# Stacking the high and low halves of a folded 33-token chunk over partitions: one or two matmuls in place of three in a Fourier transform

## The chip, the cores and the metric

The kernel runs on one NeuronCore of a Trainium2 chip. The metric is the device time of one execution in microseconds (us). Five engines work side by side, each through its own instructions in order: TensorE (PE; its weight loads are listed as PEld), VectorE (DVE), ScalarE (ACT), GpSimd (POOL) and SyncE (SP), which issues most of the DMAs.

## The reference

Attention with a causal window of 128 keys, then a mixing layer made of a two-dimensional Fourier transform (its real part is added to the input), a layer norm and a feed-forward net. There are 8 batches of 576 tokens, 8 heads of 64, model width 512, hidden width 2048.

```
scores = scale * np.matmul(q, k.transpose(0, 1, 3, 2))
bias = slopes[:, None, None] * (-np.abs(rel).astype(np.float32))[None, :, :]
mask = (rel >= 0) & (rel < window)
scores = np.where(mask, scores + bias[None], -1000000000.0)
...
attn = attn / (np.sum(attn, axis=-1, keepdims=True) + 1e-09)
return np.matmul(attn, v).astype(np.float32)
...
X = np.fft.fft(x, axis=1)
X = np.fft.fft(X, axis=2)
mixed = np.real(X).astype(np.float32)
u = x + mixed
...
un = (u - mu) / np.sqrt(var + 1e-06)
ch = np.maximum(un @ w_ch1, 0.0) @ w_ch2
return (u + ch).astype(np.float32)
```

## The kernel before

Each batch goes through three stages. **Attention** (`scores`, `halves`, `flip`, `values`) leaves an activation tile `X` of 576 tokens x 512 columns on 128 partitions. **The transform** (`fourier`) folds it by the symmetries of sine and cosine, multiplies along the tokens (`rows`, one column in `middle`) and along the columns (`cols`), and adds the result to `X`; `norm` then normalises. **The feed-forward net** (`ffn`) multiplies by two weight matrices (lines 698 and 712). The net of one batch runs beside attention and transform of the next.

Most matmuls need more precision than fp16 gives. A factor is therefore split into two fp16 numbers, a high half and a low half (what the high half misses), and a product is three matmuls: high x high, low x high, high x low.

In the transform the tokens are folded into three chunks, `KCH = (128, 128, 96)` partitions. For each chunk `fold_b` builds the sums and differences `ab`, `fold_c` writes the high halves `fh` (ACT), `fold_d` the low halves `fl` (DVE) and one column's two halves `a128`. `rows(g)` runs for four groups g of 128 columns, two with cosine and two with sine tables, and takes 3 chunks x 3 matmuls of 289 columns; `middle` takes 3 chunks x 3 matmuls of one column for each of three pieces of its output. The third chunk holds 33 tokens on partitions 0 to 32 and their 32 mirror tokens on 64 to 95; between them lies nothing of use, and the tables repeat the cosine rows and the negated sine rows for the mirror tokens.

For each of the batches 2 to 7 `batch_scales` (line 242) reads q, k and v once more ahead of attention, to find the scale of each. It takes 15 pieces of up to 512 columns through two slots: a DMA by `fetch` (line 253), a square and sum on ACT by `part` (line 257). The two slots mean that the third piece's DMA waits until the first is summed.

The work of all stages is put into a queue with due times (`put`, `after`), and the steps are called in the order of these times. The program is then built with a scheduler that orders the instructions of each engine by a timeline of its own; so a changed instruction can move others on every engine. `ffn` evicts each bank of its first product with a Relu on ACT (line 703) and a second half on DVE (line 704; shown as L158, the helper's line).

Of the kernel before, what the change touches and what calls it, by code (L numbers as in the profile page):

```python
# [11 lines left out]
F16 = mybir.dt.float16  # L12
BF16 = mybir.dt.bfloat16
I32 = mybir.dt.int32
AF = mybir.ActivationFunctionType
ALU = mybir.AluOpType
# [7 lines left out]
NS = 289  # L24
# [14 lines left out]
KCH = (128, 128, 96)  # L39
# [37 lines left out]
def attn_fft_ffn_kernel(  # L77
# [39 lines left out]
    A.dma_start(out=tab1_sb, in_=tab1)  # L117
    A.dma_start(out=tab2_sb, in_=tab2)
    A.activation(misc[:, 12:13], half[:, 0:1], AF.Exp)
    vhs = const.tile([128, 2, 2, 5, 65], F16, name="vhs")  # L120
    G.memset(vhs[:, :, :, :, 64:65].rearrange("p a b c d -> p (a b c) d"), 1.0)
    hbuf = const.tile([128, 4096], F32, name="hbuf")
# [15 lines left out]
    def view(t, off, *dims):  # L138
        return bass.AP(tensor=t.tensor, offset=t.offset + off, ap=[t.ap[0]] + [list(d) for d in dims])
# [353 lines left out]
    def fourier(b, t0):  # L493
        st = {}
# [16 lines left out]
        def fold_b(c):  # L511
            m = KCH[c]
            pm = t2k.tile([128, 1032], F32, name="pm", tag="a4", bufs=3).rearrange("p (a b) -> p a b", a=4)
            V.memset(pm[:m, :, 256:257], 0.0)
            ab = t2k.tile([128, 516], F32, name="abcd", tag="b2")[:, 0:512]
            if c < 2:
                fg = st["fg", c]
                V.tensor_tensor(pm[:, 0:2, 0:256], fg[:, :, 0:256], fg[:, :, 256:512], ALU.add)
                V.tensor_tensor(pm[:, 2:4, 0:256], fg[:, :, 0:256], fg[:, :, 256:512], ALU.subtract)
                ia, ib, ic, id_ = 0, 2, 3, 1  # L520
            else:
                X2 = st["X2"]
                V.tensor_tensor(pm[:m, 0, 0:256], X2[:m, 0:256], X2[:m, 256:512], ALU.add)
                V.tensor_tensor(pm[:m, 1, 0:256], X2[:m, 0:256], X2[:m, 256:512], ALU.subtract)
                ia, ib, ic, id_ = 0, 1, 1, 0
            pmm, abm = pm[:m], ab[:m]
            for (i, j, op, o) in ((ia, ic, ALU.add, 0), (ib, id_, ALU.subtract, 128)):
                s_ = 258 * (j - i)
                V.tensor_tensor(view(abm, o, (256, 2), (1, 128)),
                                view(pmm, 258 * i, (s_ + 1, 2), (1, 128)),  # L530
                                view(pmm, 258 * i + 256, (s_ - 1, 2), (-1, 128)), op)
            st["pm", c], st["ab", c] = pm, ab

        def fold_c(c):
            m, sc = KCH[c], st["sc"]
            fh = st["fh", c] = dft.tile([128, 512], F16, name=f"fh{c}")
            A.activation(fh[:m], st["ab", c][:m], AF.Copy, scale=sc[:m, 5:6])

        def fold_d(c):
            m, sc = KCH[c], st["sc"]  # L540
            fh, ab, pm = st["fh", c], st["ab", c], st["pm", c]
            fl = dft.tile([128, 512], F16, name=f"fl{c}")
            V.scalar_tensor_tensor(fl[:m], ab[:m], sc[:m, 5:6], fh[:m], ALU.mult, ALU.subtract)
            a128 = dft.tile([128, 2], F16, name=f"a128{c}")
            V.tensor_scalar(a128[:m, 0:1], pm[:m, 0, 128:129], sc[:m, 5:6], None, ALU.mult)
            V.scalar_tensor_tensor(a128[:m, 1:2], pm[:m, 0, 128:129], sc[:m, 5:6], a128[:m, 0:1],
                                   ALU.mult, ALU.subtract)
            st["in", c] = fh.rearrange("p (g j) -> p g j", g=4), fl.rearrange("p (g j) -> p g j", g=4), a128

        def rows(g):  # L550
            zp = st["zp", g] = bank(b)
            for c, m in enumerate(KCH):
                for p, (l, t) in enumerate(((0, 0), (1, 0), (0, 1))):
                    T.matmul(zp[:, :NS], st["in", c][l][:m, g], tab1_sb[:m, (0 if g < 2 else 2) + t, c],  # L554
                             start=(c == 0 and p == 0), stop=(c == 2 and p == 2))

        def rows_hi(g):
            zh = st["zh", g] = dft.tile([128, NS], F16, name=f"zh{g}")
# [6 lines left out]
        def middle():  # L565
            gps = st["gps"] = bank(b)
            for j, (j0, mj) in enumerate(SCH):
                for c, m in enumerate(KCH):
                    for p, (t, col) in enumerate(((0, 0), (0, 1), (1, 0))):
                        T.matmul(gps[:mj, j:j + 1], tab1_sb[:m, t, c, j0:j0 + mj], st["in", c][2][:m, col:col + 1],  # L570
                                 start=(c == 0 and p == 0), stop=(c == 2 and p == 2))

        def middle_out():
            gt = st["gt"] = small.tile([128, 2, 3], F32, name="gt")
# [52 lines left out]
        t = t0 + f * 2.6  # L627
# [135 lines left out]
def tables():  # L763
# [20 lines left out]
    def split(t):  # L784
        hi = t.astype(np.float16)
        return hi, (t - hi.astype(np.float64)).astype(np.float16)
# [10 lines left out]
    s = np.arange(NS)[None, :]  # L797
    c1, s1 = trig(t * s, 576)
    c1[289:], s1[289:] = 0.0, 0.0
    c1[320:352], s1[320:352] = c1[256:288], -s1[256:288]  # L800
    tab1 = np.empty((128, 4, 3, NS), np.float16)
    for i, x in enumerate(split(c1 * 2048) + split(s1 * 2048)):
        tab1[:, i] = x.reshape(3, 128, NS).transpose(1, 0, 2)
    j0 = np.arange(128)[:, None]
    ke, ko = np.arange(0, 257, 2)[None, :], np.arange(1, 256, 2)[None, :]
    w = np.ones((128, 1))
# [64 lines left out]
```

## Time and profile before

| | |
|---|---|
| Time, three runs | 1102.3 us median (1100.52 to 1106.19) |
| The profiled execution | 1104.11 us, of which the trace spans 1102.3 us |
| PE busy | 1056.0 us (96% of the span), 9260 matmuls |
| DVE busy | 711.4 us (65%) |
| ACT busy | 581.7 us (53%) |
| POOL busy | 19.8 us (2%) |

The share of busy time is an average over stages that have different limits. Up to some 365 us the engines wait for each other and for DMAs; after that PE is busy without a gap until shortly before the end. Matmuls are pipelined, so the duration of one overlaps the next; the chain that ended last shows what each adds.

### The profile page before, as it was taken

What the parts mean: (1) busy time and instruction counts of PE and PEld (TensorE: products, weight loads), DVE (VectorE), ACT (ScalarE), POOL (GpSimd) and SP (SyncE); (2) the same over time, 40 slices, a digit from 0 to 9 for tenths busy, and PEclk for the clock granted to TensorE, in tenths of its full rate; (3) what the DMA queues carried; (4) which work ended last, traced back from release to release, by engine and by line L of the source; (5) the groups of instructions that cost most, each with busy time, mean ns of one, the idle gap of its engine ahead of it and who ended that gap; (6) DMA issues with size and microseconds to landing.
All of it is one profiled execution on the core that took longest, in us unless ns stands there. A gap on an engine that the chain in (4) does not pass through costs nothing.

```text
span 1102.3 us, 23881 instructions
## 1 busy us (share of the span) xinstructions
PE 1056.0 (96%) x9260; PEld 738.6 (67%) x9260; DVE 711.4 (65%) x2081; ACT 581.7 (53%) x1380; POOL 19.8 (2%) x59
## 2 busy tenths in 40 slices
PE   6989989989799999999999999999999999999998
PEld 5776767565566766676757578585757676757665
DVE  5999588637766586868777576868685755262111
ACT  5867799658765465457544465457444441241000
POOL 0000000000000000000000000000000000010000
PEclk8988869999899999999999999999999999999999
DMA  9862376756767245343624154335432230020000
GB/s 367 309 204 57 114 180 168 193 156 157 142 162 193 69 101 112 73 102 83 135 74 85 42 114 92 88 78 109 110 91 37 54 82 1 20 58 11 20 11 20
DMA packets 191506, 117.81 MB, mean 107 GB/s; under 512 B 154400, under 2 KB 164128, under 8 KB 191392
## 3 DMA queue, kind: packets, MB, share of 16 engines
q1 hardware_dynamic: 190816, 114.84, 41.2%
q8 instruction: 72, 1.18, 0.5%
q10 hardware_dynamic: 576, 1.45, 0.3%
q14 instruction: 42, 0.34, 0.1%
HBM read 70.63 MB, written 9.44 MB: 73 GB/s over the span
## 4 chain that ended last, share of the span: by engine, by line
PE 71%; DMA 10%; DVE 9%; ACT 6%; issue 2%; SPq 1%; ACTq 0%; DVEq 0%
PE fp L698 28%; PE fp L712 27%; PE sp L378 5%; PE pd L554 3%; DMA wall<-q_dram 2%; ACT wall L257 2%; DMA wall<-k_dram 2%; DMA wall<-v_dram 2%; PE pv L440 1%; ACT P L158 1%; PE pd L588 1%; DVE P L390 1%; PE pv L445 1%; DMA pt<-P 1%; DVE wall L190 1%
## 5 line engine op out<-in xcount | busy, mean ns | idle before, releaser
L712 PE MATMUL fp<-wall,hbuf 128*128 128x512 f16 x1728 | 393.0, 381 | 2.1 <-DVE hbuf L158 2.1
L698 PEld LDWEIGHTS <-wall 128*128 128x128 f16 x3840 | 339.8, 99 | 61.8 <-issue 13.3
L698 PE MATMUL fp<-uT,wall 128*128 128x256 f16 x3072 | 366.2, 276 | 14.4 <-DVE hbuf L158 10.3
L712 PEld LDWEIGHTS <-hbuf 128*128 128x128 f16 x1728 | 162.6, 98 | 186.3 <-issue 7.4
L158 ACT ACTIVATE P<-P,nb 128x256 f32<-128x256 f32 x320 | 142.0, 479 | 119.6 <-DVE nb L390 119.5
L703 ACT ACTIVATE hbuf<-fp 128x512 f16<-128x512 f32 x144 | 85.1, 591 | 184.9 <-PE fp L698 184.9
L158 DVE SCALAR_TENSOR_TENSOR hbuf<-fp,hbuf 128x512 f16<-128x512 f32 x144 | 98.8, 688 | 128.6 <-ACT hbuf L703 128.1
L390 DVE CUSTOM_DVE_ANT_0 P<-sp,rg,nsl 128x256 f32<-128x256 f32 x240 | 97.6, 449 | 58.7 <-PE sp L378 50.4
L378 PE MATMUL sp<-kk,qq 64*128 64x256 f16 (+5 forms) x880 | 95.6, 294 | 6.1 <-DMA kk<-k_dram 5.2
L158 DVE SCALAR_TENSOR_TENSOR P<-P 128x256 f16<-128x256 f32 x240 | 88.3, 388 | 17.4 <-ACT P L403 16.0
L403 ACT ACTIVATE P<-P 128x256 f16<-128x256 f32 x240 | 85.6, 384 | 4.5 <-DMA pt<-P 4.1
L257 ACT ACTIVATE wall<-wall 128x512 f32<-128x512 f32 (+2 forms) x90 | 54.8, 611 | 47.1 <-DMA wall<-v_dram 16.9
L445 PE MATMUL pv<-vhs,pt 128*128 128x65 f16 x432 | 55.0, 196 | 2.9 <-DVE X L462 1.5
L446 PE MATMUL pv<-vl,pt 128*128 128x64 f16 x432 | 55.5, 194 | 0.0
L447 PE MATMUL pv<-vhs,pt 128*128 128x65 f16 x432 | 55.4, 194 | 0.0
L158 DVE SCALAR_TENSOR_TENSOR X<-fp,misc,X 128x512 f32<-128x512 f32 x32 | 23.8, 743 | 43.9 <-PE fp L712 43.6
L445 PEld LDWEIGHTS <-pt 128*128 128x128 f16 x432 | 41.1, 98 | 12.9 <-issue 4.0
L378 PEld LDWEIGHTS <-qq 64*128 64x128 f16 (+1 forms) x720 | 31.7, 99 | 24.5 <-issue 21.1
L698 PE MATMUL fp<-wall,wall 128*128 128x128 f16 x768 | 45.4, 220 | 0.1
L446 PEld LDWEIGHTS <-pt 128*128 128x128 f16 x432 | 40.7, 99 | 6.6
L440 PE MATMUL pv<-vr,pt 128*128 128x65 f32 x288 | 43.2, 305 | 0.9 <-DVE X L462 0.8
L440 PEld LDWEIGHTS pv<-vr,pt 128*128 128x128 f32 x288 | 40.9, 222 | 3.8 <-DVE X L462 1.4
(146 smaller groups left out, 1187.1 us busy)
## 6 DMA issues: line engine op xcount, KB each, us to landing
qr<-q_dram SPq DMA_DIRECT2D x32, 304.0 KB, 3.1
hbuf<-w_dram SPq DMA_DIRECT2D x16, 512.0 KB, 6.8
out_dram<-X SPq DMA_DIRECT2D x32, 256.0 KB, 2.4
wall<-v_dram SPq DMA_DIRECT2D x30, 256.0 KB, 3.0
vr<-v_dram SPq DMA_DIRECT2D x24, 320.0 KB, 3.3
kr<-k_dram SPq DMA_DIRECT2D x24, 289.0 KB, 3.2
wall<-q_dram SPq DMA_DIRECT2D x24, 256.0 KB, 2.9
wall<-k_dram SPq DMA_DIRECT2D x24, 256.0 KB, 2.9
```

Source lines behind the costliest of these rows:

```text
L158: put(now[0] + dt, lambda: f(*a, **kw))
L257: A.activation(t, t, AF.Square, accum_out=box["mx"][:, i, c:c + 1])
L378: T.matmul(sp[e][:m, col:col + n], qq[h, c0:c0 + m], keys(kk[h], ti), start=(x == 0), stop=(x == len(prods) - 1))
L390: V.tensor_tensor_reduce(pt[:m, 0:n], sp[e][:m, col:col + n], tab[:m, pc:pc + n], mul, 3.0e38, ALU.add, ALU.min, nb[:m, ti:ti + 1])
L403: A.activation(hi, P32, AF.Copy, scale=2.0 ** 14)
L440: T.matmul(pv[:, ti], pt[:, col:col + 128], ops[p][2][:, e, vc], start=first, stop=last)
L445: T.matmul(pv[:, ti], ph, vh[:, e, vc], start=first, stop=False)
L446: T.matmul(pv[:, ti, 0:D], ph, vl[:, e, vc], start=False, stop=False)
L447: T.matmul(pv[:, ti], pl, vh[:, e, vc], start=False, stop=last)
L698: T.matmul(fp[:, i * n:(i + 1) * n], w1_ap(e, c, f0 + i), uT[:, j, c, 0:n], start=(c == 0 and p == 0), stop=(c == 3 and p == 2))
L703: A.activation(ht[:, 0], fp, AF.Relu)
L712: T.matmul(op, hh[f][:, a, i * 128:(i + 1) * 128], w2_ap(e, f), start=(f == 0 and p == 0), stop=(f == 15 and p == 2))
```

## The change

The third chunk is folded once more: on DVE the 32 mirror tokens are added to the 32 tokens (cosine) or subtracted (sine), so 33 (sine: 32) tokens are left. Their high and low halves are then stacked over the partitions of one constant tile, `stack`, and the table is stacked to match. For sine the partitions hold high, high, low against table high, low, high: one matmul gives all three products. For cosine, where 33 rows don't fit three times into 32-partition steps, partitions 0 to 32 hold high and 64 to 96 low against the high table, and a second matmul of 33 partitions gives high x low table. `stack1` is the same for the column of `middle`. POOL clears both tiles once at the start.

```
+    stack = const.tile([128, 512], F16, name="stack")
+    stack1 = const.tile([128, 1], F16, name="stack1")
+    G.memset(stack, 0.0)
+    G.memset(stack1, 0.0)
...
+            if c == 2:
+                for lo, hi, op, x in ((0, 256, ALU.add, ab), (256, 512, ALU.subtract, ab), (128, 129, ALU.add, pm[:, 0])):
+                    V.tensor_tensor(x[0:32, lo:hi], x[0:32, lo:hi], x[64:96, lo:hi], op)
...
+            if c == 2:
+                ab = st["ab", c]
+                A.activation(stack[0:33], ab[0:33], AF.Copy, scale=sc[0:33, 5:6])
+                A.activation(stack[32:64, 256:512], ab[0:32, 256:512], AF.Copy, scale=sc[0:32, 5:6])
+                return
...
+            if c == 2:
+                pm, s = st["pm", c][0:33, 0, 128:129], sc[0:33, 5:6]
+                V.scalar_tensor_tensor(stack[64:97], st["ab", c][0:33], s, stack[0:33], ALU.mult, ALU.subtract)
+                V.tensor_scalar(stack1[0:33], pm, s, None, ALU.mult)
+                V.scalar_tensor_tensor(stack1[64:97], pm, s, stack1[0:33], ALU.mult, ALU.subtract)
+                return
...
         def rows(g):
             zp = st["zp", g] = bank(b)
-            for c, m in enumerate(KCH):
-                for p, (l, t) in enumerate(((0, 0), (1, 0), (0, 1))):
-                    T.matmul(zp[:, :NS], st["in", c][l][:m, g], tab1_sb[:m, (0 if g < 2 else 2) + t, c],
-                             start=(c == 0 and p == 0), stop=(c == 2 and p == 2))
+            o = 0 if g < 2 else 2
+            prods = [(st["in", c][l][:, g], tab1_sb[:, o + t, c]) for c in range(2) for l, t in ((0, 0), (1, 0), (0, 1))]
+            rest = stack[:, 128 * g:128 * g + 128]
+            for t, m in ((0, 97), (1, 33)) if g < 2 else ((2, 96), ):
+                prods.append((rest[:m], tab1_sb[:m, t, 2]))
+            for x, (l, r) in enumerate(prods):
+                T.matmul(zp[:, :NS], l, r, start=(x == 0), stop=(x == len(prods) - 1))
...
-                for c, m in enumerate(KCH):
-                    for p, (t, col) in enumerate(((0, 0), (0, 1), (1, 0))):
-                        T.matmul(gps[:mj, j:j + 1], tab1_sb[:m, t, c, j0:j0 + mj], st["in", c][2][:m, col:col + 1],
-                                 start=(c == 0 and p == 0), stop=(c == 2 and p == 2))
+                prods = [(tab1_sb[:, t, c, j0:j0 + mj], st["in", c][2][:, x:x + 1])
+                         for c in range(2) for t, x in ((0, 0), (0, 1), (1, 0))]
+                prods += [(tab1_sb[:m, t, 2, j0:j0 + mj], stack1[:m]) for t, m in ((0, 97), (1, 33))]
+                for x, (l, r) in enumerate(prods):
+                    T.matmul(gps[:mj, j:j + 1], l, r, start=(x == 0), stop=(x == len(prods) - 1))
```

**PE, the first group of columns of batch 1.** Here `rows` ends with the third chunk, whose high halves are `fh_2527` and low halves `fl_2566` (`fh_2658` is the second chunk). Before:

```order
L554 LDWEIGHTS fh_2658
L554 MATMUL pd<-tab_sb,fh_2658 128x289
L554 LDWEIGHTS fh_2527
L554 MATMUL pd<-tab_sb,fh_2527 128x289
L554 LDWEIGHTS fl_2566
L554 MATMUL pd<-tab_sb,fl_2566 128x289
L554 LDWEIGHTS fh_2527
L554 MATMUL pd<-tab_sb,fh_2527 128x289
```

And now, where line 576 is the changed `rows`, `fh_2655` the second chunk and line 720 the feed-forward net's old line 698:

```order
L576 LDWEIGHTS fh_2655
L576 MATMUL pd<-tab_sb,fh_2655 128x289
L576 LDWEIGHTS stack
L576 MATMUL pd<-tab_sb,stack 128x289
L576 LDWEIGHTS stack
L576 MATMUL pd<-tab_sb,stack 128x289
L720 LDWEIGHTS wall_109
L720 MATMUL fp<-uT,wall_109 128x256
```

The third chunk's three pairs of weight load and matmul have become two; in the two sine groups they become one.

**ACT, around the 25th to 27th eviction of the feed-forward net.** Before, the evictions (L703) stand between the last pieces of `batch_scales` (L257); counted from the start of the program, 85 pieces stand ahead of the first L703 below and 89 ahead of the third:

```order
L257 ACTIVATE wall_105,mx<-wall_105 128x512 x3
L537 ACTIVATE fh_4366<-abcd,sc 128x512
L257 ACTIVATE wall_105,mx<-wall_105 128x264
L703 ACTIVATE hbuf<-fp 128x512
L257 ACTIVATE wall_105,mx<-wall_105 128x512 x2
L703 ACTIVATE hbuf<-fp 128x512
L559 ACTIVATE zh_4474<-pd 128x289
L257 ACTIVATE wall_105,mx<-wall_105 128x512 x2
L703 ACTIVATE hbuf<-fp 128x512
L257 ACTIVATE wall_105,mx<-wall_105 128x512
```

Now the same evictions are L725 and the pieces L261 (L407 and L162 are steps of attention):

```order
L261 ACTIVATE wall_109,mx<-wall_109 128x384
L162 ACTIVATE P<-P,nb 128x256
L162 ACTIVATE P<-P,nb 96x256
L407 ACTIVATE P<-P 128x256
L162 ACTIVATE P<-P,nb 128x256
L725 ACTIVATE hbuf<-fp 128x512
...
L261 ACTIVATE wall_109,mx<-wall_109 128x512
L407 ACTIVATE P<-P 96x256
L725 ACTIVATE hbuf<-fp 128x512
L580 ACTIVATE zh_4462<-pd 128x289
L725 ACTIVATE hbuf<-fp 128x512
L261 ACTIVATE wall_109,mx<-wall_109 128x512 x2
```

The 25th, 26th and 27th eviction now stand behind 80, 82 and 82 of the 90 pieces, where it was 85, 87 and 89. From the first transform's folds to about here the order differs on PE, DVE, ACT and SP. Behind it, attention and feed-forward matmuls follow each other on PE as before but for a few exchanges.

## Rows read from the trace of the kernel before

**Rows 1.** Busy time of each engine in six stretches of the span. Columns: stretch, its length, then busy us and instructions of PE, PEld, DVE, ACT and POOL, granted TensorE clock (1 is full speed), DMA share, GB/s.

```profile
0.00:103.00 103.00, 87.89 (x656) 69.67 (x657) 87.17 (x276) 71.21 (x149) 1.19 (x10) 0.92 0.70 247
103.00:200.00 97.00, 90.98 (x634) 68.61 (x634) 75.75 (x231) 83.58 (x202) 1.87 (x7) 0.81 0.59 150
200.00:320.00 120.00, 104.05 (x940) 72.31 (x939) 73.92 (x235) 81.99 (x217) 2.56 (x9) 0.96 0.64 161
320.00:365.00 45.00, 41.14 (x306) 25.87 (x306) 27.23 (x70) 25.96 (x69) 0.10 (x1) 0.96 0.66 166
365.00:950.00 585.00, 583.46 (x5574) 400.66 (x5572) 407.05 (x1203) 289.19 (x687) 11.19 (x27) 1.00 0.37 82
950.00:1102.30 152.30, 148.52 (x1159) 101.53 (x1156) 40.31 (x73) 29.74 (x61) 2.93 (x5) 1.00 0.08 22
```

**Rows 2.** Waits of PE from 365 us to the end: who waited for whom, us in total, times, longest.

```profile
PE fp L698 <- DVE X L158: 0.9, 1, 0.9
PE pv L445 <- DVE X L462: 0.3, 1, 0.3
PE fp L698 <- DVE hbuf L158: 0.2, 1, 0.2
```

**Rows 3.** The chain that ended last, from 940 us on: start, us that it adds, engine, tile and line, number of instructions.

```profile
951.55 1.12 PE pd L554 x9
...
959.79 0.74 PE pd L570 x27
...
1056.72 20.72 PE fp L712 x96
...
1088.16 10.38 PE fp L712 x48
...
1098.56 0.75 DVE ut L158
```

**Rows 4.** The chain that ended last, from 326 to 366 us.

```profile
350.74 3.19 DMA wall<-v_dram
353.95 0.73 ACT wall L257 x2
354.70 2.55 DMA wall<-v_dram
357.27 0.73 ACT wall L257 x2
358.02 2.50 DMA wall<-v_dram
360.55 0.72 ACT wall L257 x2
...
364.28 1.28 PE pd L554 x9
```

**Rows 5.** The pieces of `batch_scales` on ACT from 329 to 362 us: count, duration in ns (min/median/max), first and last start.

```profile
L257 ACT ACTIVATE wall<-wall x17: 405/629/632, 329.1 to 360.5; 128x512 f32<-128x512 f32 x15, 128x384 f32<-128x384 f32 x1, 128x264 f32<-128x264 f32 x1
```

**Rows 6.** ACT in order of time around 354 us (start, us, engine, line, operation, what ended the idle time before it), and PE behind it.

```profile
353.95 0.63 ACT L257 ACTIVATE wall<-wall 128x512 f32<-128x512 f32 x1 [3.02 <-DMA wall<-v_dram]
354.48 0.19 ACT L257 ACTIVATION_READ_ACCUMULATOR wall<-wall 128x1 f32 x1
354.64 0.63 ACT L257 ACTIVATE wall<-wall 128x512 f32<-128x512 f32 x1
355.18 0.19 ACT L257 ACTIVATION_READ_ACCUMULATOR wall<-wall 128x1 f32 x1
355.27 0.58 ACT L703 ACTIVATE hbuf<-fp 128x512 f16<-128x512 f32 x1
...
356.63 1.47 PE L698 MATMUL fp<-uT,wall 128*128 128x256 f16 x12 [1.69 <-DVE hbuf L158]
```

**Rows 7.** Groups of instructions, shapes apart, of the third chunk and of those nearest to the new ones: line, engine, operation, shape, count, busy us, mean ns of one, idle time before.

```profile
L554 PE MATMUL pd<-tab_sb,fh 128*128 128x289 f16 x116 | 27.6, 292 | 2.4 <-DVE zl L563 2.4
L554 PE MATMUL pd<-tab_sb,fh 96*128 96x289 f16 x58 | 15.9, 293 | 0.0
L537 ACT ACTIVATE fh<-abcd,sc 96x512 f16<-96x512 f32 x8 | 5.7, 717 | 23.8 <-DVE abcd L529 23.8
L403 ACT ACTIVATE P<-P 128x256 f16<-128x256 f32 x144 | 56.8, 405 | 3.6 <-DMA pt<-P 3.4
L545 DVE TENSOR_SCALAR a<-pm,sc 96x1 f16<-96x1 f32 x8 | 1.6, 198 | 0.0
```

**Rows 8.** DVE in order of time in the second half of a transform, where some operations cross from one group of 32 partitions to another (L614 to L617).

```profile
520.39 0.42 DVE L606 TENSOR_TENSOR ds<-ab 33x257 f32<-33x257 f32 x1
520.73 0.41 DVE L607 TENSOR_TENSOR ds<-ab 33x256 f32<-33x256 f32 x1
521.17 0.42 DVE L614 TENSOR_TENSOR ds<-ab 32x257 f32<-32x257 f32 x1
```

**Rows 9.** PE in order of time in batch 0's transform: start, us, line, operation.

```profile
119.07 0.45 PE L554 MATMUL pd<-tab_sb,fl 96*128 96x289 f16 x1
119.31 0.45 PE L554 MATMUL pd<-tab_sb,fh 96*128 96x289 f16 x1
119.55 0.45 PE L554 MATMUL fp<-tab_sb,fl 128*128 128x289 f16 x1
```

**Rows 10.** Stretches in which PE idled or its clock was lowered, columns as in rows 1.

```profile
100.00:103.70 3.70, 1.87 (x11) 1.08 (x11) 3.70 (x18) 3.56 (x7) 0.00 (x0) 1.00 0.37 91
103.70:120.80 17.10, 17.06 (x65) 11.90 (x62) 12.07 (x32) 10.96 (x22) 0.10 (x1) 0.50 0.21 67
120.80:141.30 20.50, 18.76 (x176) 15.39 (x175) 12.15 (x45) 17.67 (x61) 0.20 (x2) 1.00 0.48 136
141.30:161.70 20.40, 17.98 (x76) 13.92 (x76) 17.55 (x65) 20.40 (x44) 1.57 (x4) 0.50 0.77 162
280.00:300.00 20.00, 14.18 (x135) 10.01 (x134) 14.55 (x58) 16.37 (x36) 1.24 (x2) 0.87 0.67 113
```

More of the change, by code (lines that the diff above doesn't have):

```diff
@@ L799, in tables @@
     c1[289:], s1[289:] = 0.0, 0.0
-    c1[320:352], s1[320:352] = c1[256:288], -s1[256:288]
     tab1 = np.empty((128, 4, 3, NS), np.float16)
@@ L803, in tables @@
         tab1[:, i] = x.reshape(3, 128, NS).transpose(1, 0, 2)
+    (ch, cl), (sh, sl) = split(c1[256:289] * 2048), split(s1[256:288] * 2048)
+    tab1[:, :, 2] = 0.0
+    tab1[0:33, 0, 2], tab1[64:97, 0, 2], tab1[0:33, 1, 2] = ch, ch, cl
+    tab1[0:32, 2, 2], tab1[32:64, 2, 2], tab1[64:96, 2, 2] = sh, sl, sh
     j0 = np.arange(128)[:, None]
```

## The prediction, made before the changed kernel was run

> **What bounds the kernel now.** I first read the busy time by stretches [rows 1], to see where an engine has no slack. From 365 to 950 us PE is busy 583.5 of 585.0 us at full clock, and from 950 us to the end 148.5 of 152.3. DVE is busy 407 and ACT 289 of the same 585 us. Then the waits of PE behind 365 us [rows 2]: 1.4 us altogether. Then the chain that ended last [rows 3]: behind 940 us it is made of PE's matmuls, up to one DVE operation at the end. So behind 365 us a matmul that goes is time that goes.
>
> Ahead of that it is different. From 200 to 365 us PE is busy 104.05 of 120 and 41.14 of 45 us [rows 1], so it idles 16.0 and 3.9 us. The chain there alternates between DMAs into `wall` and the sums on ACT that read them (L257), until PE takes over at about 364 us [rows 4]. These are the pieces of `batch_scales`: the last 17 of them start between 329.1 and 360.5 us [rows 5], 31.4 / 16 = 1.96 us apart. How that reaches PE shows at 354 us [rows 6]: ACT stands 3.02 us at a sum whose DMA hasn't landed, the Relu eviction (L703) queued behind it runs at 355.27, and PE has waited 1.69 us for the second half of that bank (hbuf, DVE). From 103.7 to 120.8 and from 141.3 to 161.7 us, moreover, PE runs at a granted clock of 0.50, which is 1.2 of 2.4 GHz; ahead of the first fall it was busy 1.87 of 3.7 us [rows 10].
>
> **What is removed on PE.** In each batch `rows` has 4 x 9 = 36 matmuls of 289 columns; now two cosine groups have 8 and two sine groups 7, so 30. `middle` goes from 27 to 24. The chain gives the price without the overlap: nine of `rows` add 1.12 us, 0.124 each, and 27 of `middle` 0.74 us, 0.027 each [rows 3]. Does a matmul on 97 or 33 partitions cost the same? That needs one fact of the trace: on 96 partitions 293 ns against 292 on 128 [rows 7]. So a batch saves 6 x 0.124 + 3 x 0.027 = 0.83 us.
>
> How much of it counts? Batches 3 to 7 lie behind 365 us whole. Of batch 2 the third group of four runs at 364.28 us [rows 4], so I count half. That is 5.5 x 0.83 = 4.6 us. Batches 0, 1 and half of 2 are transformed where DMA and ACT carry the chain. The bounds are nothing and all: 2.5 x 0.83 = 2.1 us, and for batch 0, in part at half clock, where two of these matmuls start 0.24 us apart [rows 9], up to 0.7 more. From 326 to 364 us the chain holds no PE at all, so I take near the lower bound: 0.3 us.
>
> The Trainium skill, "TensorE: Matmul & The Clock Gate", section on the back-to-back issue gap, gives a sustained spacing in real kernels of 81 ns at 128 columns and 131 at 512, which at 289 would be an estimated 102 ns. By that page the six matmuls would be worth 0.61 us per batch instead of 0.75. This trace doesn't agree: 96 matmuls of 512 columns add 20.72 us, 216 ns each [rows 3], and the sum above keeps 0.124.
>
> **What is added.** DVE gets two additions of 32 x 256 and one of 32 x 1 per batch. The nearest row is a 32 x 257 one at 0.42 us [rows 8]; the small one I take by a one-column operation at 0.2 us [rows 7]. That is 1.0 us per batch. The nearest rows also show that crossing partitions costs a little: L607 starts 0.34 us behind L606, but L614, which writes to another group of 32, starts 0.44 behind L607 [rows 8]. With five such crossings or so per batch, 0.1 each, DVE gets 1.5 us, 12 us in all. ACT gets one copy of 32 x 256, by the nearest row 0.4 us [rows 7]; the shorter copy of 33 instead of 96 partitions stays at 0.72, since this is the time of 512 columns [rows 7]. POOL's two clears are hidden: POOL is busy 1.2 us in the first 103 [rows 1]. The DMAs stay the same in number.
>
> The Trainium skill, "VectorE: DVE Perf Modes", section on two Vector instructions with no wait between them, speaks against this change: it says that an instruction whose operands start in another 32-partition group than the previous ones' is held until all earlier ones are done. By that rule, with which the 0.34 and 0.44 us agree, the new operations (whose two inputs lie in different groups) cost the 0.5 us per batch that I added, and without it they would cost 1.0.
>
> Behind 365 us that is covered: DVE has 178 idle us of 585 [rows 1] and PE waits 1.4 us for anything [rows 2]. If the cover were gone it would cost 5.5 x (1.5 + 0.4) = 10.5 us at most. The third chunk is folded first and multiplied last, so the folds of the two other chunks lie between. In batch 0 it is not covered: from 100.0 to 103.7 us DVE is busy all of it [rows 10]. Bounds: 0 and 1.9 us; I take 0.5.
>
> **What is moved.** The scheduler reorders PE, DVE, ACT and SP's queue of DMAs from the first folds to some 365 us; POOL's order stays but for its two clears. The place that matters is ACT around the 25th to 27th eviction: these stood behind 85, 87 and 89 of the 90 pieces of `batch_scales`, and now behind 80, 82 and 82. At 1.96 us each, the 27th could come 7 x 1.96 = 13.7 us earlier. But the pieces that it passes aren't gone; what comes behind them (evictions 28 to 30, the next q, k and v) waits for them instead. What can be gained is idle time of PE: 3.9 us around this place, 19.9 from 200 us on. What can be lost is a second stall like the one from 280 to 300 us, where PE is busy 14.18 of 20: 5.8 us [rows 10]. I take a gain of half the idle time at this place, 1.9 us, since rows 6 show that very wait.
>
> **Sum.** -4.6 - 0.3 + 0.5 - 1.9 = -6.3 us. The profiled execution took 1104.1 us (span 1102.3), so it would take 1097.8. The median of the runs is 1.8 us lower, 1102.3, so I predict 1096.0.
>
> **Rivals.**
> - Given back. The matmuls go, but the new order has one more stall of rows 10's size: -4.6 - 0.3 + 0.5 + 5.8 = +1.4, 1103.7; with a part of it 1099 to 1104. For it: DMA and ACT set the pace up to 364 us, and more pieces now remain behind the 27th eviction. Against: the pieces are as many as before.
> - Filled. The earlier evictions let PE use half of all its idle time from 200 us on, 9.9 instead of 1.9 us: 1088. For it: the waits at evictions are of this kind [rows 6]. Against: not all idle time lies at evictions.
> - Slower: one more stretch at half clock. Around 103 us the order of PE changes too, and there PE is so thinly fed that the clock fell twice, for 17.1 and 20.4 us [rows 10]. A third stretch of 20.4 us with PE busy would cost 10.2: without the gain of the order 1102.3 - 4.4 + 10.2 = 1108.1. It decides from 4.4 us of lost PE time, 9 us at half clock. Against: part of the lost time would be idle anyway.
> - The change doesn't do what it says: if 97 partitions were slower to load or multiply, the four cosine matmuls per batch would have to take over twice as long to eat the gain. Rows 7 speak against it; I give it no chance of its own.
>
> **How the numbers follow.** 0.5% of this time, about what its measurement can tell from no change, is 5.5 us: the line lies at 1096.8, so the forecast sits just past it. Forecast (1091 to 1099): 0.47, of which 0.32 is past the line. Given back: 0.24. Filled: 0.17. Slower: 0.12. Faster is 0.32 + 0.17 = 0.49, same 0.15 + 0.24 = 0.39, slower 0.12. The range leaves out the slower case and the lower third of the filled one: 1087 to 1104. The forecast's own range is 1091 to 1099.
>
> **What would show it.** Right: `rows` with 240 and `middle` with 192 matmuls, at 0.124 and 0.027 us in the chain; from the start of batch 3's attention to the end 4.2 us less (5 x 0.83); PE waits behind 365 us still under 3 us; PE idle from 200 to 365 us down by some 2 us. Wrong: PE waiting for `stack`; new waits for hbuf behind the last pieces of `batch_scales`; a third stretch at half clock; a part behind 365 us that shrank by less than 4 us.

## The result, and the profile after

The changed kernel takes 1111.5 us (median of 8 runs, 1109.96 to 1112.22) against 1104.2 us for the kernel before in the same comparison: a ratio of 1.0064, with a 95% interval of 1.0045 to 1.0084. Predicted were 1096.0 us and a range up to 1104. The forecast had the wrong sign. A second comparison (e15 below) gave 1113.1 against 1108.2, a ratio of 1.0035 (1.0011 to 1.0059).

The profiled execution of the changed kernel took 1109.96 us, with a span of 1108.2; the sum of the prediction gave 1097.8 for it. Where do these 12.2 us lie? The same stretches as in [rows 1] (PE, PEld, DVE, ACT, POOL, granted clock, DMA share, GB/s):

```profile
103.00:200.00 97.00, 88.36 (x565) 69.14 (x566) 65.73 (x203) 74.84 (x176) 1.87 (x7) 0.72 0.44 119
200.00:320.00 120.00, 108.49 (x955) 73.38 (x954) 86.95 (x273) 87.96 (x234) 3.49 (x9) 0.94 0.72 173
320.00:365.00 45.00, 38.12 (x286) 23.27 (x284) 25.09 (x63) 22.25 (x60) 0.10 (x1) 0.92 0.58 158
365.00:950.00 585.00, 583.38 (x5540) 398.89 (x5538) 416.25 (x1224) 298.41 (x713) 11.24 (x27) 1.00 0.38 85
950.00:1108.20 158.20, 154.39 (x1195) 105.66 (x1194) 41.86 (x76) 30.70 (x63) 2.93 (x5) 1.00 0.08 23
```

Two things stand out. From 103 to 200 us the granted clock is 0.72 where it was 0.81, with 69 matmuls fewer done. And behind 365 us PE is as full as before, at full clock, and still what remains did not get shorter. Its waits there are still 1.6 us (who waited for whom, us, times, longest), so nothing new is waited for:

```profile
PE fp L720 <- DVE X L162: 0.9, 1, 0.9
PE fp L720 <- DVE hbuf L162: 0.4, 2, 0.2
PE pv L449 <- DVE X L466: 0.3, 1, 0.3
```

As a yardstick I use the start of the feed-forward net's Relu evictions on ACT, counted from the first, because they come in the same order in all the kernels. The 37th stands at 430.05 us before and at 436.13 after: 6.1 us late. The 139th stands at 1054.14 and 1060.01: 5.9 late. So from batch 3 to the end, where 5 x 0.83 = 4.15 us should have been saved, the change saved 0.2; everything else was lost ahead of 430 us. The 37th and the 139th, first before, then after:

```profile
430.05 0.60 ACT L703 ACTIVATE hbuf<-fp 128x512 f16<-128x512 f32 x1 [0.47 <-PE fp L698]
1054.14 0.60 ACT L703 ACTIVATE hbuf<-fp 128x512 f16<-128x512 f32 x1 [2.02 <-PE fp L698]
```

```profile
436.13 0.60 ACT L725 ACTIVATE hbuf<-fp 128x512 f16<-128x512 f32 x1 [0.48 <-PE fp L720]
1060.01 0.60 ACT L725 ACTIVATE hbuf<-fp 128x512 f16<-128x512 f32 x1 [2.02 <-PE fp L720]
```

**Why nothing is saved behind 430 us.** The chain that ended last (start, us added, tile and line, count), to be read beside [rows 3]:

```profile
953.74 1.09 PE pd L576 x8
954.83 3.27 PE fp L720 x29
958.10 0.87 PE pd L576 x7
...
965.95 0.99 PE pd L593 x24
```

Seven products (a sine group) add 0.87 us, 0.124 each, as predicted. But eight products (a cosine group) add 1.09 instead of 0.99, the 29 feed-forward products behind them 3.27 instead of the 3.17 that 29 of them add elsewhere, and the 24 of `middle` 0.99, more than the 27 before (0.74). The weight loads of that cosine group show which product it is:

```profile
954.19 0.10 PEld L576 LDWEIGHTS <-stack 97*128 97x128 f16 x1
954.53 0.09 PEld L576 LDWEIGHTS <-stack 33*128 33x128 f16 x1 [0.24 <-issue]
954.76 3.06 PEld L720 LDWEIGHTS <-wall 128*128 128x128 f16 x29
```

Loads follow each other every 0.12 us, each covered by the matmul ahead of it. The load over 97 partitions does too. The one over 33 stands 0.24 us idle first, though it waits for nothing, and is itself no longer than the others (0.09 us); the next load then starts 0.23 us behind it.

**What was lost ahead.** In stretches of 4 us around batch 0's transform (columns as above):

```profile
116.00:120.00 4.00, 4.00 (x17) 3.28 (x17) 0.94 (x4) 2.07 (x4) 0.00 (x0) 0.50 0.29 87
120.00:124.00 4.00, 4.00 (x13) 1.39 (x13) 1.97 (x5) 1.96 (x6) 0.00 (x0) 0.50 0.00 0
124.00:128.00 4.00, 4.00 (x16) 2.94 (x15) 1.54 (x5) 1.73 (x5) 0.00 (x0) 0.50 0.43 131
...
136.00:140.00 4.00, 4.00 (x22) 3.99 (x21) 0.00 (x0) 1.15 (x7) 0.00 (x0) 0.50 0.41 115
140.00:144.00 4.00, 4.00 (x33) 3.23 (x33) 1.61 (x5) 3.10 (x11) 0.07 (x1) 0.58 0.33 87
```

PE is busy all the time, but at clock 0.50 (1.2 of 2.4 GHz), from 105.8 to 143.4 us. Before, this stretch ended at 120.8 [rows 10]. The eviction of the last of batch 0's three `cols` pieces, called its last `cols` eviction below, starts at 149.1 us instead of 139.0: 10 us late.

So there are two theories to test. First: the product over 33 partitions costs its own saving, because its load is not covered. Second: batch 0's transform now stays at half clock for 37.5 us, and that is the larger part. The rivals: the new order of the instructions costs the time, or the added work on DVE and ACT does.

### The profile page after: what moved, and what is told of

It reads as the page before. It is cut to its first block, busy times and chain, and to the rows that moved or that the text cites. A ratio compares the mean times of both kernels' runs of the same rounds, so it can differ in the third digit from the quotient of the medians.

```text
span 1108.2 us, 23754 instructions
## 1 busy us (share of the span) xinstructions
PE 1061.6 (96%) x9188; PEld 740.5 (67%) x9188; DVE 722.2 (65%) x2105; ACT 584.8 (53%) x1388; POOL 21.4 (2%) x61
## 4 chain that ended last, share of the span: by engine, by line
PE 78%; DVE 8%; DMA 7%; ACT 4%; issue 2%; SPq 0%; POOL 0%; ACTq 0%; DVEq 0%
PE fp L720 31%; PE fp L734 27%; PE sp L382 6%; PE pv L444 3%; PE pd L576 3%; DMA wall<-q_dram 2%; DMA wall<-v_dram 2%; PE fp L303 2%; PE sp L425 1%; PE pd L610 1%; DMA uT<-un 1%; ACT wall L261 1%; DMA pt<-P 1%; PE pv L449 1%; DVE P L394 1%
## 5 line engine op out<-in xcount | busy, mean ns | idle before, releaser
L162 ACT ACTIVATE P<-P,nb 128x256 f32<-128x256 f32 x320 | 142.0, 479 | 107.1 <-DVE nb L394 107.0
L725 ACT ACTIVATE hbuf<-fp 128x512 f16<-128x512 f32 x144 | 84.9, 590 | 186.6 <-PE fp L720 186.6
L162 DVE SCALAR_TENSOR_TENSOR hbuf<-fp,hbuf 128x512 f16<-128x512 f32 x144 | 98.8, 687 | 127.5 <-ACT hbuf L725 127.1
L162 DVE SCALAR_TENSOR_TENSOR P<-P 128x256 f16<-128x256 f32 x240 | 88.7, 390 | 23.4 <-ACT P L407 21.9
L407 ACT ACTIVATE P<-P 128x256 f16<-128x256 f32 x240 | 85.2, 383 | 2.0 <-DMA pt<-P 1.7
L261 ACT ACTIVATE wall<-wall 128x512 f32<-128x512 f32 (+2 forms) x90 | 54.6, 607 | 50.2 <-DMA wall<-v_dram 23.2
L162 DVE SCALAR_TENSOR_TENSOR X<-fp,misc,X 128x512 f32<-128x512 f32 x32 | 23.8, 745 | 43.6 <-PE fp L734 43.6
L444 PE MATMUL pv<-vr,pt 128*128 128x65 f32 x288 | 47.7, 326 | 4.0 <-issue 2.3
L444 PEld LDWEIGHTS pv<-vr,pt 128*128 128x128 f32 x288 | 45.1, 242 | 7.6 <-issue 4.9
```

The costliest lines, as they stand in the source:

```text
L162: put(now[0] + dt, lambda: f(*a, **kw))
L261: A.activation(t, t, AF.Square, accum_out=box["mx"][:, i, c:c + 1])
L407: A.activation(hi, P32, AF.Copy, scale=2.0 ** 14)
L444: T.matmul(pv[:, ti], pt[:, col:col + 128], ops[p][2][:, e, vc], start=first, stop=last)
L725: A.activation(ht[:, 0], fp, AF.Relu)
```

## Experiments

Half-clock sums below are 2 x (1 - granted clock) x span of a run. For the profile of the changed kernel the mean clock of 0.961 gives 86 us; its stretches at 0.50 add up to 85.3. The clock of a run is given to 0.001, so such a sum is good to about 1 us. A ratio is always to the runs of the kernel before in the same comparison; their median was 1106.6 us beside e1, e2, e5 and e8, 1107.2 beside e9 to e12, and 1108.2 beside e13 to e16. The three comparisons ran on three chips.

### Undoing one part, or doing one alone

**e1: all stacked products over 128 partitions** (the rows more are zeros in the table). The order on all engines is that of the changed kernel.

```
-for t, m in ((0, 97), (1, 33)) if g < 2 else ((2, 96), ):
+for t, m in ((0, 128), (1, 128)) if g < 2 else ((2, 128), ):
...
-prods += [... for t, m in ((0, 97), (1, 33))]
+prods += [... for t, m in ((0, 128), (1, 128))]
```

> The changed kernel with one difference: every matmul of the stacked chunk runs over all 128 partitions (the rows beyond 97 or 33 are zero in the tables and finite in the tile). All instructions stand in the same order as in the changed kernel on every engine. Theory A: in the changed kernel the 33-partition weight load can't overlap the matmul ahead of it, nor the next load the 33-partition matmul, which there makes a cosine group 1.19 us from its first to the next matmul (1.12 before with nine products) and the middle column 1.09 (0.84 before). Then a cosine group takes 8 x 0.124 = 0.99 here, the middle column 24 x 0.027 = 0.66 to 0.75, a batch 0.7 to 0.8 us less than in the changed kernel: 4 us less behind 365 us, 1107 to 1108 us. Rival B: what is missing behind 365 us lies in the order; then the time stays at 1111.5.

1101.6 us (1098.76 to 1111.25, 12 runs), 0.9965 of before (0.9941 to 0.999): faster than both. In its chain the eight products add 0.99 and the 24 of `middle` 0.67:

```profile
944.91 0.99 PE pd L576 x8
...
956.91 0.67 PE pd L593 x24
```

From the 37th to the 139th eviction it takes 619.4 us, against 624.1 before: 4.65 us, somewhat more than the 4.15 predicted. The added work on DVE and ACT and the order are those of the changed kernel, so neither of them ate the saving. But against before it stands some 10 us better than the changed kernel does, which is more than loads can give: the stretch at half clock in batch 0 was 20.5 us long in its profile instead of 37.5.

**e2: the change only from batch 2 on**, batches 0 and 1 by the old products.

```
+        new = b >= 2
...
-            if c == 2:
+            if c == 2 and new:
```

> The stacked form only in batches 2 to 7; batches 0 and 1 keep the old form (three products per chunk, no second fold), and the table is longer by one column block. Theory A: the 6 to 10 us that the changed kernel loses between 100 and 365 us come from how batch 0's and 1's matmuls are ordered, which keeps PE at half clock for 37.5 us from 106 us on, where before had 17.1 and full clock after that. With the old form the first stretch at half clock is again near 17 us and the time is that of before less 6 x 0.11: 1103 to 1105. Rival B: the loss comes from the new instructions in batches 2 to 7; then 1109 to 1111.

1108.0 us (1105.93 to 1114.73, 10 runs), 1.0025 (1.0006 to 1.0044). Batch 0's `cols` came on time (the last eviction at 139.1 us), and from the 37th to the 139th eviction it took 623.1 us, a saving of 1.0. The first stretch at half clock is 20.5 us long, as Theory A has it, but the time is above A's 1103 to 1105 (with before at 1104): the 37th eviction is still 3.6 us late. Its order ahead of 365 us differs from before's too.

**e8: the folds alone.** The kernel before with the three DVE additions of each batch, written to partitions that nothing reads, and all its products.

```
+            if c == 2:
+                for lo, hi, op, x in ((0, 256, ALU.add, ab), (256, 512, ALU.subtract, ab), (128, 129, ALU.add, pm[:, 0])):
+                    V.tensor_tensor(x[96:128, lo:hi], x[0:32, lo:hi], x[64:96, lo:hi], op)
```

> The kernel before with the three additions of the second fold on VectorE in each batch, written to partitions 96 to 127, which nothing reads; all products as before. Theory A (the order and the clock): the scheduler orders 100 to 365 us anew; the time goes with the length of the half-clock stretches, and behind 365 us it stays as before: 1104 if these stay at some 69 us in sum, up to 1112 if they grow as in the changed kernel (86 us). Rival B (the work added on VectorE itself costs): 1.0 to 1.5 us per batch that isn't covered, spread over all batches, 1108 to 1114 with half-clock stretches as before.

1117.6 us (1113.09 to 1124.57, 4 runs), 1.0107 (1.0073 to 1.0141). Behind the 37th eviction it takes 623.1 us, no more than before: the added DVE work is hidden there. The loss of 11.4 us is complete at 430 us, and 3.8 us of it stand at batch 0's last `cols` eviction; the rest came with an order of instructions that differs again. The time is above both forecasts. In its profile the half-clock stretches add up to 69.5 us, about as before (68), but PE idles 28.4 us from 200 to 365 us instead of 19.8: so the loss lies in waits, with no change in the products and little in the clock.

**e12: the cut alone.** The kernel before with 8, 8, 7 and 7 products and 24 in `middle`; folds and copies as before, 96 partitions in the third chunk's products.

```
-                for p, (l, t) in enumerate(((0, 0), (1, 0), (0, 1))):
+                n = 3 if c < 2 else 2 if g < 2 else 1
+                for p, (l, t) in enumerate(((0, 0), (1, 0), (0, 1))[:n]):
...
```

> The kernel before with the products cut alone: of the third chunk's three products one is left out in the cosine groups and in middle, two in the sine groups, so part of the sum is missing; folds, copies and subtractions as before, 96 partitions in each product that is left. Theory: behind 430 us it saves 0.83 us in each of five batches, 4.2 us, since 96 partitions load as fast as 128 (0.10 us); ahead of that the order between 100 and 365 us changes as in all other runs, and with it 0 to 10 us go either way. Time 1096 to 1108 with before at 1104. Rival: products cut save nothing unless their neighbours are full, and nothing is gained behind 430 us.

1114.4 us (1110.35 to 1118.46, 7 runs), 1.0068 (1.0041 to 1.0095), above the range of 1096 to 1108. Behind the 37th eviction the theory holds: 620.4 us, a saving of 3.7, and its chain has the predicted prices:

```profile
961.34 0.99 PE pd L555 x8
...
973.24 0.66 PE pd L572 x24
```

But at the 37th eviction it is 17.1 us late. Of these 7.5 stand at batch 0's last `cols` eviction, behind 34.1 us at half clock from 105.4 us; the rest comes up to 365 us. So this cut, with nothing added on any engine, loses more ahead of 430 us than it saves behind; its order differs from before's, too.

### What the 33-partition product costs

**e9: 64 partitions in place of 33**, in `rows` and in `middle`, order as in the changed kernel.

```
-((0, 97), (1, 33))
+((0, 97), (1, 64))
```

> The changed kernel with one size changed: the second stacked product of each cosine group, and of each column of middle, runs over 64 partitions in place of 33 (the 31 more hold zeros in the table). All five engines have the same order as in the changed kernel. If it is the shortness of the 33-partition operand that keeps its weight load out of the cover of the product before, and half of the partitions are enough, the cosine group goes from 1.19 us to about 1.0 and the run comes out like the one with all partitions, 10 us under the changed kernel. If a load must only differ from its neighbours (97 ahead of it, 128 behind) to lose its cover, the group stays at 1.19 us and the time within 2 us of the changed kernel.

The half was not enough. 1112.7 us (1102.23 to 1117.78, 10 runs), 1.003 (0.9998 to 1.0063). The gap stays, first in the loads, and so do the prices, second in the chain:

```profile
948.29 0.10 PEld L576 LDWEIGHTS <-stack 97*128 97x128 f16 x1
948.63 0.09 PEld L576 LDWEIGHTS <-stack 64*128 64x128 f16 x1 [0.24 <-issue]
```

```profile
947.84 1.09 PE pd L576 x8
...
960.06 0.99 PE pd L593 x24
```

**e13: 65 partitions in place of 33**, in `rows` and in `middle`, order as in the changed kernel.

```
-((0, 97), (1, 33))
+((0, 97), (1, 65))
```

> As the run with 64 partitions, with one partition more: 65 in the second stacked product of each cosine group and of each column of middle; same order on all engines. With 33 and with 64 partitions the weight load starts 0.24 us late and the cosine group takes 1.09 us of the chain, with 96, 97 and 128 there is no such gap and it takes 0.99. Theory: the load of a product over no more than half of the partitions is not covered by the product ahead of it. Then 65 gives 0.99 us and 24 products of middle 0.67 in place of 0.99, and behind 430 us the run gains 3.5 to 4.5 us as with 128. Rival: the step lies between 65 and 96, or a load of another height than its neighbours' is what counts: then 1.09 us and nothing gained behind 430 us.

One partition more, and the gap is gone:

```profile
956.04 0.99 PE pd L576 x8
...
968.05 0.67 PE pd L593 x24
```

The steady part saves 3.9 us (620.15 from the 37th to the 139th eviction). The whole took 1108.6 us (1097.91 to 1111.73, 10 runs), 0.9992 of before (0.9966 to 1.0018), for a reason that the next runs show.

The other kernels bear it out. From the 37th to the 139th eviction, in the profile of each (before: 624.1 us):

| second stacked product, batches 3 to 7 | us |
|---|---|
| 33 partitions: changed kernel, e15, e10, e16 | 623.9, 623.7, 623.2, 623.4 |
| 64 partitions: e9 | 623.5 |
| 65 partitions: e13 | 620.2 |
| 128 partitions: e1, e11, e14 | 619.4, 620.3, 619.7 |

All of these share the changed kernel's order behind batch 0. Of the others, e2 and e5 keep the 33 partitions in an order of their own and take 623.1 and 622.0 us, and e8, which removes no product, takes 623.1. So another order moves this yardstick by some 1 to 2 us; the 3.4 us between 64 and 65 partitions stand within one order.

The trace of before had shown this, in rows that I didn't read: attention's scores multiply over 64 partitions. The group of their loads has 20.9 us of idle time put down to issue, and in order of time a group of them stands between two gaps, at its begin and at the return to 128:

```profile
L378 PEld LDWEIGHTS <-qq 64*128 64x128 f16 x576 | 23.5, 94 | 24.0 <-issue 20.9 <-ACT kk L353 0.2
```

```profile
443.00 0.36 PEld L378 LDWEIGHTS <-qq 64*128 64x128 f16 x7 [0.21 <-issue]
443.55 2.52 PEld L698 LDWEIGHTS <-wall 128*128 128x128 f16 x24 [0.18 <-issue]
```

The Trainium skill, "TensorEngine Tiling (Array Packing)", section "Key Properties", states that a change of the tiling mode (whether the array works as one of 128 rows or as tiles of fewer) drains TensorE. That a product over 64 or fewer partitions is such a change is not shown here; a boundary between 64 and 65 agrees with it. The runs put the price, in and out, at full clock, at 0.20 us for a lone product of `rows` and 0.11 for one of `middle` (0.32 / 3). The Trainium skill, "TensorE: Matmul & The Clock Gate", section "LDWEIGHTS (loading the stationary operand)", says that a load over 32 partitions takes as long as one over 128. That holds for the load itself (93 ns over 33, 99 over 128) and doesn't tell of the gap ahead of it.

### What batch 0 costs

**e10: 128 partitions in batch 0 alone. e11: in batches 1 to 7 alone.** Both in the order of the changed kernel.

```
-((0, 97), (1, 33))
+((0, 128 if b == 0 else 97), (1, 128 if b == 0 else 33))
...
+((0, 128 if b > 0 else 97), (1, 128 if b > 0 else 33))
...
```

> The changed kernel with the stacked products over 128 partitions in batch 0 alone; batches 1 to 7 as changed; same order on all engines. Theory: of the 10 us that full partitions gave, about 6 come from the stretch at half clock that batch 0's groups stand in (37.5 us in the changed kernel, 20.5 with full partitions). Then this run has a stretch near 20 us there, batch 0's cols come some 8 us earlier than in the changed kernel, nothing is gained behind 430 us, and the time is about 5 to 6 us under the changed kernel's. Rival: the stretch came out shorter by chance and the gain is the sum of all groups' shorter loads: then it stays near 37 us and the time is at most 1.5 us under the changed kernel's.

> The complement: the stacked products over 128 partitions in batches 1 to 7, the 97 and 33 of the changed kernel in batch 0; same order on all engines. Theory: the long stretch of 37 us at half clock stays, and 7 batches save 0.7 us each: 4 to 5 us under the changed kernel, of which 3.5 lie behind 430 us. Rival (the gain is all in the loads, the clock a bystander): 9 us under the changed kernel.

e10 took 1105.3 us (1103.84 to 1115.77, 10 runs), 1.0008 of before (0.9978 to 1.0039); e11 1111.3 us (1109.59 to 1114.42, 10 runs), 1.004 (1.0024 to 1.0056). In its profile e10 saves nothing to speak of behind the 37th eviction (0.9 us) and has batch 0's last `cols` eviction at 141.7 us; e11 saves 3.8 behind it and has that eviction at 149.4. So the 128 partitions in batch 0 work on the stretch, those in the other batches on the steady part. Only the size for e11 is smaller than expected: it stands 4.1 us above before, the changed kernel 7.3 and 4.9 above it in its two comparisons.

But e10's ten runs do not stand around one time. Six lie between 1103.8 and 1105.5 us with 68 to 77 us at half clock in sum, and a seventh at 1111.7 with 76; three lie between 1111.9 and 1115.8 with 87 to 96. The same holds for e9 (three runs from 1102.2 to 1105.3 with 62 to 66 us, seven from 1111.3 up with 80 to 96) and for e1. So it seems that the end of the stretch comes early or late from run to run, and that a kernel only has odds. One profile doesn't tell them. That a large sum means a long stretch in batch 0 is read off the profiles of the kernels in this order, one of each: the four with a sum of 83 us or more have a first stretch there of 37.5 to 40.9 us, the five with 77 or less one of 10.2 to 20.5. For the other runs only the sum is known.

**e15: the changed kernel once more**, beside e13, e14 and e16.

> The changed kernel itself, for a comparison on one chip with the runs beside it. Expected 1.0064 of before again, all its runs with over 80 us at half clock in sum. If some of its runs come out near 1104 us with 60 to 75 us at half clock, the long stretch in batch 0 is an outcome that can go either way for this kernel too, and not a property of the 33-partition products.

1113.1 us (1104.78 to 1116.75, 10 runs). Two of its runs, at 1104.8 and 1106.0, have 66 and 57 us at half clock, the eight others 82 to 98. So, by these sums, the long stretch is no fixed property of the 33-partition products; they only make it likely. The eight others have a median of 1113.7: the long stretch costs some 8 us. The two short runs stand 3.4 and 2.2 us under the median of before beside them.

**e16: two copies of the first product ahead of each group of batch 0**, partitions as changed. **e14: the same copies, and 128 partitions everywhere.** Their order is the same on all engines, and from batch 0's end on about that of the changed kernel.

```
+            for _ in range(2 if b == 0 else 0):
+                T.matmul(zp[:, :NS], prods[0][0], prods[0][1], start=True, stop=True)
```

> The changed kernel with two copies of the first product put ahead of each of the four groups of batch 0 (0.25 us more work each at full clock, 0.5 us at half): 33-partition products stay. From batch 0's end on, the order is that of the changed kernel; within batch 0 a few turn and value products move. Theory: the engine's clock comes back early in batch 0 when its groups keep it busier; then the stretch at half clock that begins near 105 us is 3 to 20 us long in place of 37.5 and the time falls to about 1104. Rival: the long stretch comes with the 33-partition loads: it stays, time 1111 to 1113.

> The same two copies with the stacked products over 128 partitions; order on all engines as in the run with 33-partition products and two copies. If full partitions and more work in batch 0 both keep the stretch short, all runs stand near 1100 us, where with full partitions alone 3 of 12 stood at 1107 to 1111. Behind 430 us it gains 4 to 4.6 us like the other run with 128 partitions. Rival: the copies are only work on the path and cost 2 us (8 x 0.25), with as many long runs as before: median 1103.

e16 took 1107.9 us (1103.68 to 1116.2, 10 runs), 1.0002 (0.9973 to 1.0031), halfway between theory and rival: three of its runs stand at 1115 to 1116. e14 took 1100.9 us (1098.6 to 1107.14, 8 runs), 0.9948 (0.9921 to 0.9975), the fastest of all. In both profiles the first stretch at half clock in batch 0 is 10.2 us long. e16 saves 0.7 us behind the 37th eviction, e14 4.4.

**e5: four copies**, partitions as changed.

> The changed kernel with four more copies of the first product in each of batch 0's four groups (their sum is started anew behind them, so the result is the same): 16 more matmuls of 289 columns, 2.0 us at full and 3.9 at half clock. The order may change with them. Theory A (the clock): the longer bursts bring the clock back earlier, the half-clock stretch from 106 us on is 17 to 24 us instead of 37.5, which gives back 7 to 10 us of PE time: 1103 to 1108. Rival B (the clock isn't it): 2 to 4 us more than the changed kernel, 1113 to 1116.

1124.1 us (1123.44 to 1125.02, 4 runs), 1.0161 (1.0146 to 1.0175). The first stretch was 3.4 us long and batch 0's last `cols` eviction stood at 139.6 us, on time. But with four copies the order behind batch 0 changed as well, and from 200 to 320 us PE was busy only 87.57 of 120 us:

```profile
200.00:320.00 120.00, 87.57 (x791) 59.11 (x789) 74.39 (x230) 78.28 (x207) 2.88 (x9) 0.86 0.65 165
```

PE's three largest waits from 200 to 365 us:

```profile
PE pv L449 <- DMA pt<-P: 9.2, 3, 6.2
PE fp L722 <- DVE hbuf L162: 7.7, 3, 6.5
PE pd L612 <- ACT ab L624: 6.3, 2, 5.9
```

In all PE idles there for 39.3 us, where the changed kernel has 18.4, and 41.0 us run at half clock instead of 20.5. At batch 0's last `cols` eviction e5 was 9.5 us ahead of the changed kernel, at the 37th eviction 17.0 us behind it: the new order lost far more than the clock had given.

Counted over all runs of the kernels that share the changed kernel's order behind batch 0, with 79.5 us or more at half clock in sum as "long" (none of these runs lies between 77.2 and 79.5):

| batch 0's groups | long runs |
|---|---|
| 33, 96 and 97 partitions (changed kernel, e15, e11) | 26 of 28 |
| 64, 96 and 97 (e9) | 7 of 10 |
| 65, 96 and 97 (e13) | 9 of 10 |
| 33, 96 and 97 and two copies (e16) | 3 of 10 |
| 128 (e1, e10) | 6 of 22 |
| 128 and two copies (e14) | 1 of 8 |

The kernel before has 3 long ones of the 80 runs that stand beside these experiments. e13 and e10 make a close pair: from 106.6 to 123.5 us their profiles have the same matmuls at the same times to 0.01 us, PE is busy without a gap from 108 us on, and no load of a stacked product waits in batch 0 of either. Two things differ: the partitions of the stacked products, of which four start up to 123.5 us, and the fall of the clock, at 106.2 us in e13 and 106.5 in e10 (up to there e10 runs 0.14 us later). First e13, then e10:

```profile
116.00:120.00 4.00, 4.00 (x18) 3.38 (x18) 1.37 (x4) 2.50 (x5) 0.00 (x0) 0.50 0.25 62
120.00:124.00 4.00, 4.00 (x14) 2.16 (x14) 1.97 (x5) 1.87 (x5) 0.00 (x0) 0.50 0.07 25
124.00:128.00 4.00, 4.00 (x16) 2.97 (x15) 1.54 (x5) 1.77 (x5) 0.00 (x0) 0.50 0.43 131
```

```profile
116.00:120.00 4.00, 4.00 (x18) 3.38 (x18) 1.36 (x4) 2.50 (x5) 0.00 (x0) 0.50 0.26 64
120.00:124.00 4.00, 4.00 (x15) 2.08 (x14) 1.97 (x5) 1.89 (x5) 0.00 (x0) 0.55 0.07 24
124.00:128.00 4.00, 4.00 (x29) 3.26 (x29) 2.08 (x8) 2.96 (x8) 0.00 (x0) 1.00 0.41 131
```

In e10 the clock is back at 1.00 from 123.6 us, in e13 only from 143.8. In one pair of profiles this could be chance, or go with the moment of the fall, which no run sets apart; the long runs are what speaks for the partitions. They are 9 of 10 against 3 of 10, but on different chips. On e10's chip e11, which differs from it only in the batches that have the 128 partitions, has 10 of 10, and e9 7 of 10. So the partitions of batch 0's products change the odds; for 65 alone, without the late loads of 33 and 64, it rests on two chips. Why products over fewer partitions make a late return likelier was not shown.

## Why the prediction was wrong, point by point

- **Removed on PE: the step that failed first.** "Does a matmul on 97 or 33 partitions cost the same?" was answered with the row for 96 [rows 7]. It holds for 97 and for everything from 65 up; 33 is on the other side of a boundary. Each 33-partition product of `rows` costs 0.20 us more (0.10 in its own group, 0.10 in the piece behind it), and the six transitions of `middle` 0.32 in all: 2 x 0.20 + 0.32 = 0.72 of the 0.83 us per batch. Of 4.15 us over batches 3 to 7, 0.2 came. The 0.124 and 0.027 us per removed product were right, as e1, e11, e12, e13 and e14 show (3.7 to 4.65 us). The last rival named exactly this, with 97 in place of 33, and got no chance, by the row for 96. A row below 65 partitions was at hand in the scores.
- **Slower by one more stretch at half clock: the rival that came.** It was priced at 10.2 us and given 0.12, and the sum took nothing for it. No third stretch came, but the first went from 17.1 to 37.5 us, at the place named. At the 37th eviction the change should have been 2.1 us early (-0.4 -0.3 +0.5 -1.9) and was 6.1 late. These 8.2 us and the 4.0 us missing behind are the 12.2 us between sum and profile. Over the profiles a long stretch costs about 8 us: in the changed kernel's order the 37th eviction is 6.1, 9.6, 10.0 and 11.6 us late with it (changed kernel, e15, e11, e13), 0.5, 1.2 and 2.0 us without (e9, e1, e10). But the 8.2 us here are not all its doing, and that the two numbers agree is luck. By the kernels without it, 4.1 to 5.6 us of the 6.1 go with the stretch; of the rest, 1.9 is the reorder gain of the next point, and 0.7 to 2.2 us have no cause that was shown. The argument against this rival, that part of the lost time would be idle anyway, held only in part: PE was busy throughout the stretch, but of the 10 us at batch 0's last `cols` eviction 6.1 are left at the 37th.
- **The reorder gain of 1.9 us: not seen.** The 25th to 27th eviction did move ahead of pieces of `batch_scales`, yet the 25th eviction started at 357.6 us instead of 350.4. From 200 to 365 us PE idled 18.4 instead of 19.8 us, but 20.5 us of this stretch ran at half clock instead of 13.7, and the longest single wait for hbuf was 6.6 us instead of 3.8. In e9's profile, whose batch 0 had the early end, the 25th eviction stands at 350.6, 0.2 behind before's: the move by itself is worth nothing that these runs can tell.
- **DVE and ACT: right.** The additions took 413 ns each (0.42 taken), DVE's busy time from 365 to 950 us rose by 9.2 us (5.5 batches at 1.5 were taken), and ACT's added copy took 507 ns instead of 0.4 us; all of it was hidden behind 365 us, as e1 and e8 show.

```profile
L538 DVE TENSOR_TENSOR abcd<-abcd 32x256 f32<-32x256 f32 x16 | 6.6, 413 | 0.5
L546 ACT ACTIVATE stack<-abcd,sc 32x256 f16<-32x256 f32 x8 | 4.1, 507 | 0.2
```

- **Filled and given back** did not come: PE's idle time from 200 to 365 us went down by 1.4 us, where the one needed 9.9 less and the other 5.8 more. What stays open is how much of e8's, e12's and e5's losses ahead of 430 us is the order itself: every edit that changes the number of instructions gave another order there, and at the 37th eviction these kernels stand 11.4, 17.1 and 23.1 us behind before. The order of before could not be kept with the new products, so this was not separated.

## What to carry to other kernels

Price a matmul by a row on the same side of 64 partitions: here a lone product over 33 or 64 between fuller ones lost its cover and cost more than the product that it replaced, while padding its operand with zeros to 65 or 128 cost nothing. Where a stretch runs at half clock, removing matmuls from it is not free: look at what brings the clock back there before anything is taken away, and read the odds from many runs, since one profile shows one outcome. And a saving that is certain in the steady part (4 us here) is smaller than what a reordered start-up can lose (up to 23 us).

## What the runs showed of the hardware

- A weight load over 33 or 64 partitions behind one over 97 waited 0.24 us; over 65, 96, 97 or 128 there was no gap (changed kernel, e9, e13, e1).
- By the half-clock sums, the clock came back to 1.00 early in some runs of a program and late in others: late in 16 of 18 runs of the changed kernel, in 6 of 22 of e1 and e10. Products over 128 partitions in batch 0 changed these odds (e10 3 of 10, e11 10 of 10 on the same chip), and so did 8 products more there (e16, 3 of 10).
